# The order of two DMA issues ahead of the first projection, and one more matmul of ones, in a gated-mix kernel

## The chip, the cores and the metric

The kernel runs on one core of one Trainium2 chip. The metric is device time in microseconds (us). The engines are TensorE (PE; its weight loads are shown apart, as PEld), VectorE (DVE), ScalarE (ACT), GpSimd (POOL) and SyncE (SP). SP and ACT issue the DMAs here, each on a queue of its own: in the profile SP's is q1 and ACT's is q10, and both move their packets over the same 16 DMA engines.

## What is computed

Two mixers of a sequence of 2048 tokens of width 512 and a gate between them:

```python
x = A_x                                            # (1, 2048, 512), bf16
g = sigmoid((x * gate_w).sum(-1, keepdims=True))
# A: attention with 32 heads of 16, over 8 earlier tokens at a step of 2
qkv = x @ wqkv                                     # wqkv: (512, 1536)
a = softmax(q . k at positions s, s-2, ..., s-14) @ v, then @ wo
# B: a MLP over tokens
h = layernorm(x)                                   # over the width
u = gelu(einsum("bsd,sf->bdf", h, w1) + b1)        # f = 1792
b = transpose(einsum("bdf,fs->bds", u, w2) + b2)
out = g * a + (1 - g) * b
```

## The kernel before, in words

All of SBUF is one tensor, `arena`, cut into regions: X (x, tokens on the partitions, 16 tiles of 128 tokens), XT (x transposed, four chunks of 128 of the width, 2048 tokens), WQKV, W1W, Q5, K5, V5 and others. PSUM is `ps`, eight banks of 512 columns; banks 0 to 3 are called acc0 to acc3, banks 4 to 7 lg4 to lg7.

PE's work, in order of time: the projections of Q, K and V (L617), the attention's sums over heads (L696, twice), the first layer of the MLP (L810), its second layer (L860) and the output projection (L876). VectorE takes the statistics of the layer norm (L572 on), the products of Q and K (L688), the softmax and the products with V (L795, L798), and the last combination (L897). ACT brings PE's results out of PSUM (L625 and L628 for the projections).

Every operation is given to a small planner (`_Sched`): `add` for an engine's operation, with what it reads and writes, an estimated duration and a priority, and `dma` for a transfer on an engine's queue. The planner sorts each engine's list by estimated start, and puts semaphore waits where one engine's operation depends on another's or on a DMA. `lands` on a DMA is an estimate of when its data is there, for the planner alone; `order` fixes a sequence without a wait. Everything on an engine is then executed in the order of its list.

What the change touches is the start. Time zero is the span's start.

- **ACT's queue.** `d_xp` (line 479, issued by line 429) loads the *plain columns* of block 0: the first 128 columns of x for tokens 0 to 511, into XP, with tokens on the partitions, 128 KB. Behind it `ld_w(0, 0, 1, "act")` (line 481, issued by line 429) loads *Wq's first quarter*: rows 0 to 127 of wqkv, the 512 columns of Q, 128 KB. After these ACT loads a table and does the eviction of line 553.
- **SP's queue.** `ld_xt0` (line 473) loads columns 128 to 511 of x for tokens 0 to 511 with a transposing DMA, 384 KB, into chunks 1 to 3 of XT. Behind it come Wq's second, third and fourth quarter (128 KB each), Wk in two halves (256 KB each), x's first tiles, then the next transposing load (line 460), and so on.
- **PE.** `warm1` is five matmuls of ones by ones with 512 columns, `warm2` one with 256 columns, into bank 7 (line 536; both operands are constants of 1.0 and nothing reads the result; in this text they are the *matmuls of ones*). Then `tr0` and `tr1` (line 544) transpose the four 128 by 128 pieces of XP by a matmul with the identity into banks 5 and 6, and `warm3` is one more of line 536. Bank 5 is brought into chunk 0 of XT by ACT (`ev_tra`, line 553) and bank 6 by VectorE (`ev_trb`, line 555).
- **The first projections** (line 617). They go by quarters of the contracted width: four matmuls of 512 columns, one for each of Q's four column groups, with chunk 0 of XT and Wq's first quarter; then four with chunk 1 and the second quarter; four with chunk 2, four with chunk 3; then sixteen for K in two halves. A step waits for its chunk and its quarter. The first step so needs the plain columns, transposed and evicted, and Wq's first quarter; the second needs `ld_xt0` and the second quarter.

Of the kernel before, what the change touches and what calls it, by code (L numbers as in the profile page):

```python
# [333 lines left out]
def bass_gated_mix__sliding_local_dilated__mixer_token_mlp__prompt_kernel(nc, A_x, A_wqkv, A_wo, B_x, B_w1, B_b1, B_w2, B_b2, gate_w, out, dbg=None):  # L334
    with contextlib.ExitStack() as es:
# [79 lines left out]
        A = sch.add  # L415
# [12 lines left out]
        def mk_dma(dst, src):  # L428
            return lambda e: e.dma_start(dst, src)  # L429
# [3 lines left out]
        def throttle():  # L433
            return [init_dmas[-5]] if len(init_dmas) >= 5 else []

        def prev_dma():
            return [init_dmas[-1]] if init_dmas else []

        def ld_x(t0, n, q="sp"):
            ds = sch.dsem("x%d" % t0)  # L440
            op = sch.dma(q, mk_dma(X[:, t0:t0 + n, :], xv[:, t0:t0 + n, :]), n * 128 * D * 2, ds,
                         writes=["x%d" % t for t in range(t0, t0 + n)], deps=throttle() if q == "sp" else [], after=prev_dma() if q == "sp" else [], name="d_x%d" % t0)
            if q == "sp":
                init_dmas.append(op)
            return op

        def ld_w(tn, d0, n, q="sp"):
            ds = sch.dsem("wqkv%d_%d" % (tn, d0))
            op = sch.dma(q, mk_dma(WQKV[:, d0:d0 + n, tn * D:(tn + 1) * D], wqkv_v[:, d0:d0 + n, tn * D:(tn + 1) * D]),
                         n * 128 * D * 2, ds, writes=["wqkv%d_%d" % (tn, dt) for dt in range(d0, d0 + n)],  # L450
                         deps=throttle() if q == "sp" and n == 4 else [], after=prev_dma() if q == "sp" else [],
                         issue=0.65 if n == 4 else 0.45, name="d_wp%d_%d" % (tn, d0))
            if q == "sp":
                init_dmas.append(op)
            return op
# [14 lines left out]
        def ld_xt0():  # L470
            ds = sch.dsem("xt0")
            dst = XT[:, 1:4, 0:512]
            op = sch.dma("sp", lambda e: e.dma_start_transpose(dst, x2d[0:512, 128:512]), 512 * 384 * 2, ds, issue=1.25,
                         writes=XT0[1:4], after=prev_dma(), name="d_xt0")
            init_dmas.append(op)
            return op

        XP = view("OUTS", BF16, [(128, 4), (1, 128)])
        d_xp = sch.dma("act", mk_dma(XP, xv[:, 0:4, 0:128]), 512 * 128 * 2, sch.dsem("xp"), writes=["outs0"], issue=0.4, name="d_xp")

        first_loads = [ld_w(0, 0, 1, "act"), ld_xt0(), ld_w(0, 1, 1), ld_w(0, 2, 1), ld_w(0, 3, 1), ld_w(1, 0, 2), ld_w(1, 2, 2),
                       ld_x(0, 2)]
        ld_xt(1)
        first_loads.append(init_dmas[-1])
        for op_, t_ in zip(first_loads, (3.4, 4.6, 5.0, 5.4, 5.8, 6.6, 7.4, 8.2, 10.6)):
            op_.lands = t_
            op_.deps.clear()
        d_xp.lands = 3.1
        first_loads[0].order.add(d_xp)
        init_dmas[:] = [first_loads[1]] + first_loads[5:]  # L490
        ld_x(2, 2)
        ld_x(4, 4)
# [7 lines left out]
        def ld_w1(j):  # L500
# [4 lines left out]
            if j < 4:  # L505
# [8 lines left out]
                       writes=["wo"], deps=throttle(), after=prev_dma(), name="d_wo")  # L514
# [4 lines left out]
        for i_, (v_, n_) in enumerate(((B_b1, NFT), (B_b2, NST))):  # L519
            vr = v_.rearrange("(t q j) -> q t j", q=4, j=32)  # L520
            for q_ in range(4):
                sch.dma("sp", mk_dma(psub(BR, 32 * q_, n_, 32 * i_, [(1, 32)]), vr[q_]), n_ * 64, ds_b, reads=["br"],
                        writes=["br_%d_%d" % (i_, q_)], deps=throttle(), after=prev_dma(), name="d_b_%d_%d" % (i_, q_), issue=0.45)
        d_w1.append(ld_w1(3))
        A("dve", lambda e: e.transpose(out=BT, in_=BR), 0.2, reads=["br_%d_%d" % (i_, q_) for i_ in range(2) for q_ in range(4)],
          writes=["btc"], name="t_b")
# [5 lines left out]
        def f_warm(n, w_=D):  # L532
            def fn(e):
                ins = None
                for _ in range(n):
                    ins = e.matmul(ps[:, 7, 0:w_], lhsT=CONE[:, 0:128], rhs=CONE[:, 0:w_], start=True, stop=True)
                return ins
            return fn

        def f_tr(h):  # L540
# [4 lines left out]
                return ins  # L545
            return fn

        A("pe", f_warm(5), 2.13, writes=["lg7_0", "lg7_1"], name="warm1", prio=-100)
        w2_ = A("pe", f_warm(1, 256), 0.2, writes=["lg7_0", "lg7_1"], name="warm2", prio=-100)
        ta_ = A("pe", f_tr(0), 0.215, reads=["outs0", "ident"], writes=["lg5_0", "lg5_1"], after=[w2_], name="tr0", prio=-100)  # L550
        tr_ = A("pe", f_tr(1), 0.215, reads=["outs0", "ident"], writes=["lg6_0", "lg6_1"], after=[ta_], name="tr1", prio=-100)
# [2 lines left out]
          writes=["xt0_0"], name="ev_tra", prio=0)  # L554
        A("dve", lambda e: e.tensor_copy(out=XT[:, 0, 256:512], in_=ps[:, 6, 0:256]), 0.35, reads=["lg6_0", "lg6_1"],
          writes=["xt0_0b"], name="ev_trb", prio=0)
# [76 lines left out]
        for (b0, d0, d1, s0, s1) in ((0, 0, 1, 0, 512), (0, 1, 2, 0, 512), (0, 2, 3, 0, 512), (0, 3, 4, 0, 512), (4, 0, 2, 0, 512), (4, 2, 4, 0, 512)):  # L633
            for b in range(b0, b0 + 4):
# [3 lines left out]
                                 writes=fbn[b], after=[last_main[0]], name="pf_%s%d_%d_%d" % (tnames[tn], dl, d0, s0))  # L638
                last_main[0].order.add(w3_)
        for b, (tn, dl) in enumerate(first):  # L640
            A("act", f_evq(tn, dl, 0, b), 0.52, reads=fbn[b] + (["k5pad"] if tn == 1 else []),
              writes=["%s5_%d_0" % (tnames[tn], dl)], name="ev_%s%d_0" % (tnames[tn], dl), prio=0)
# [7 lines left out]
        for (tn, dl, sb) in seq_proj:  # L650
# [4 lines left out]
                             writes=["acc%d" % bank], after=[last_main[0]], name="pj_%s%d_%d" % (tnames[tn], dl, sb), prio=0)  # L655
            A("act", f_evq(tn, dl, sb, bank), 0.62, reads=["acc%d" % bank] + (["k5pad"] if tn == 1 else ["v5pad"] if tn == 2 else []),
              writes=["%s5_%d_%d" % (tnames[tn], dl, sb)], name="ev_%s%d_%d" % (tnames[tn], dl, sb), prio=0)
# [11 lines left out]
                writes=["xa"] + ["wqkv%d_%d" % (tn, dt) for tn in range(3) for dt in range(4)], name="d_xa")  # L669
        for t in range(NST):  # L670
# [5 lines left out]
          writes=["th"], name="g_tanh", prio=0)  # L676
# [31 lines left out]
        for wh in range(2):  # L708
# [6 lines left out]
            for (dl, c0, nc_) in pieces:  # L715
# [5 lines left out]
                  writes=wr, name="qkm_%d_%d_%d" % (wh, dl, c0), prio=0)  # L721
            rd = sum([pbn(b_) for b_ in bufs], []) + PBX[wh] + ["rp"]
            for wl in range(4):
                qop = A("pe", f_qkr(list(enumerate(bufs)), (wl,)), 0.92, reads=rd, writes=["lg%d_0" % (4 + wl), "lg%d_1" % (4 + wl)],
                        name="qkr_%d_%d" % (wh, wl), prio=-100 + wl, delay=BURST_DELAY)
                A("act", (lambda wh_, wl_: (lambda e: e.activation(out=ATT[:, :, 4 * wh_ + wl_, :], in_=ps[:, 4 + wl_, :].rearrange("p (h c) -> p h c", h=2), func=AF.Copy)))(wh, wl),  # L726
                  0.55, reads=["lg%d_0" % (4 + wl), "lg%d_1" % (4 + wl)], writes=["lw%d" % (4 * wh + wl)],
                  name="lev_%d_%d" % (wh, wl), prio=0)
# [60 lines left out]
        for k_, u in enumerate(USEQ):  # L789
# [7 lines left out]
            for (nm, n_, du) in (("ava", 4, 2.25), ("avb", 2, 1.2)):  # L797
                A("dve", (lambda pv_, n__: (lambda e: e.tensor_tensor(out=pv_[:, 0:n__], in0=pv_[:, 0:n__], in1=pv_[:, n__:2 * n__], op=ALU.add)))(pv, n_),  # L798
                  du, writes=[pn], name="%s_%d" % (nm, u))
# [27 lines left out]
        for ft in range(NFT):  # L827
# [6 lines left out]
              name="gel_%d" % ft, prio=0)  # L834
# [84 lines left out]
        for i in range(NST):  # L919
# [4 lines left out]
            elif i > 1:  # L924
# [6 lines left out]
              name="t1_%d" % i, prio=0)  # L931
# [119 lines left out]
```

## Time and profile before

| | |
|---|---|
| median of 3 runs | 167.92 us (167.65 to 168.38) |
| the profiled execution | 168.55 us |
| its span in the profile | 167.3 us |
| PE busy | 162.1 us, 97% of the span |
| DVE busy | 151.3 us, 90% |
| ACT busy | 75.1 us, 45% |
| first matmul of ones | starts 0.84 us |
| first transposing matmul (L544) | starts 3.33 us |
| first projection (L617) | starts 5.61 us |

Every line of a timeline gives start, length, engine, line, operation and the names of what it writes and reads; in square brackets stands how long the engine idled before it and what ended that. A line with "x9" merges nine instructions in a row. "DMA ... us to landing" counts from the start of the issuing instruction to the last of the DMA's semaphore updates. [...]

### The profile page before, as it was taken

How to read it: one execution, taken by the hardware profiler on the slowest of the kernel's cores; microseconds unless marked ns; L12 is line 12 of the kernel's file. 1: busy time of each engine (PE TensorE's matmuls, PEld its weight loads, DVE VectorE, ACT ScalarE, POOL GpSimd, SP SyncE). 2: the span in 40 equal slices, each digit the busy share in tenths (PEclk: the TensorE clock that was granted, in tenths of full speed). 3: DMA queues.
4: the chain of work that ended last, by engine and by line, in shares of the span. 5: the costliest groups of instructions: out<-in, count | busy, mean ns of one | idle time of the engine just before them, and what ended most of it. 6: DMA issues, size and time to landing. Idle time of an engine off the chain costs nothing.

```text
span 167.3 us, 2136 instructions
## 1 busy us (share of the span) xinstructions
PE 162.1 (97%) x845; PEld 77.5 (46%) x859; DVE 151.3 (90%) x154; ACT 75.1 (45%) x116; POOL 0.7 (0%) x8
## 2 busy tenths in 40 slices
PE   7699999999999999999999999999999999999994
PEld 2355555554454444444444444444444444444463
DVE  1055999999999999999999999999999999999896
ACT  3077688889899818793131121131231321310100
POOL 1000000000000000000000000000000000000000
PEclk9999999999999999999999999999999999999999
DMA  5999999959003846996779926462672570000454
GB/s 135 327 268 216 314 316 290 303 165 308 2 0 97 311 116 179 307 290 155 181 189 340 339 76 142 113 187 71 181 218 83 138 223 0 0 0 0 157 190 159
DMA packets 47625, 29.64 MB, mean 177 GB/s; under 512 B 9856, under 2 KB 46464, under 8 KB 47616
## 3 DMA queue, kind: packets, MB, share of 16 engines
q1 hardware_dynamic: 45120, 24.85, 54.4%
q10 hardware_dynamic: 2496, 4.66, 10.2%
q8 instruction: 7, 0.11, 0.3%
q14 instruction: 2, 0.02, 0.0%
HBM read 21.24 MB, written 2.10 MB: 140 GB/s over the span
## 4 chain that ended last, share of the span: by engine, by line
PE 91%; DMA 3%; DVE 2%; ACT 2%; issue 1%; ACTq 0%
PE ps L860 29%; PE ps L810 29%; PE ps L617 23%; PE ps L876 6%; PE ps L696 4%; DMA arena<-in_A_wqkv_dram 3%; DVE arena L897 2%; ACT L585 1%; ACT arena L628 1%; ACTq L429 0%; ACT arena L585 0%
## 5 line engine op out<-in xcount | busy, mean ns | idle before, releaser
L860 PE MATMUL ps<-arena 128*128 128x512 bf16 x220 | 48.5, 379 | 0.2
L810 PE MATMUL ps<-arena 128*128 128x512 bf16 x219 | 48.2, 379 | 0.4 <-issue 0.2
L617 PE MATMUL ps<-arena 128*128 128x512 bf16 x188 | 41.4, 379 | 1.6 <-DMA arena<-in_A_wqkv_dram 1.3
L688 DVE TENSOR_TENSOR arena<-arena 128x4096 bf16<-128x4096 bf16 (+1 forms) x12 | 35.5, 2998 | 2.5 <-ACT arena L628 2.1
L795 DVE TENSOR_TENSOR arena<-arena 128x8192 bf16<-128x8192 bf16 x8 | 35.0, 4419 | 0.0
L860 PEld LDWEIGHTS ps<-arena 128*128 128x128 bf16 x224 | 21.9, 98 | 26.4
L810 PEld LDWEIGHTS ps<-arena 128*128 128x128 bf16 x224 | 21.8, 98 | 26.6 <-ACT arena L726 0.4
L617 PEld LDWEIGHTS ps<-arena 128*128 128x128 bf16 x192 | 21.6, 113 | 21.5 <-issue 1.8
L928 ACT ACTIVATE arena<-ps,arena 128x512 bf16<-128x512 f32 x16 | 12.5, 778 | 39.4 <-PE ps L860 39.4
L798 DVE TENSOR_TENSOR arena<-arena 128x4096 bf16<-128x4096 bf16 (+1 forms) x16 | 27.0, 1751 | 0.0
L628 ACT ACTIVATE arena<-ps 128x512 bf16<-128x512 f32 x32 | 18.6, 596 | 4.5 <-PE ps L617 4.5
L831 ACT ACTIVATE arena<-ps,arena 128x512 bf16<-128x512 f32 x14 | 9.6, 687 | 22.2 <-PE ps L810 16.6
L572 DVE BATCH_NORM_STATS2 arena<-arena 128x6 f32<-128x512 bf16 x16 | 10.0, 682 | 6.1 <-DMA arena<-in_A_x_dram 6.1
L876 PE MATMUL ps<-arena 128*128 128x512 bf16 (+1 forms) x79 | 14.1, 336 | 0.1
L897 DVE SCALAR_TENSOR_TENSOR arena<-ps,arena 128x512 bf16<-128x512 f32 (+1 forms) x20 | 11.5, 637 | 0.9 <-PE ps L876 0.7
L596 ACT ACTIVATE arena<-arena 128x512 bf16<-128x512 bf16 x16 | 12.2, 804 | 0.0
L625 ACT ACTIVATE arena<-ps 128x512 bf16<-128x512 f32 x16 | 9.0, 597 | 6.2 <-PE ps L617 6.1
L876 PEld LDWEIGHTS ps<-arena 128*128 128x128 bf16 x80 | 7.8, 98 | 6.2
L672 DVE SCALAR_TENSOR_TENSOR arena<-arena 128x512 bf16<-128x512 bf16 x16 | 10.1, 689 | 0.0
L742 DVE TENSOR_TENSOR arena<-arena 128x512 bf16<-128x512 bf16 (+4 forms) x11 | 7.3, 667 | 0.6 <-ACT arena L761 0.2
L696 PE MATMUL ps<-arena 128*32 128x512 bf16 x128 | 7.3, 380 | 0.0
L726 ACT ACTIVATE arena<-ps 128x512 bf16<-128x512 f32 x8 | 4.7, 592 | 4.6 <-PE ps L696 4.6
(42 smaller groups left out, 40.0 us busy)
## 6 DMA issues: line engine op xcount, KB each, us to landing
arena<-in_B_w_dram SPq DMA_DIRECT2D x7, 1024.0 KB, 8.5
arena<-in_B_w_dram SPq DMA_DIRECT2D x8, 896.0 KB, 5.2
arena<-arena ACTq DMA_DIRECT2D x32, 128.0 KB, 2.9
arena<-in_A_x_dram SPq DMA_DIRECT2D x4, 512.0 KB, 6.1
out_dram<-arena SPq DMA_DIRECT2D x14, 128.0 KB, 1.7
arena<-in_A_x_dram SPq DMA_DIRECT2D x1, 1536.0 KB, 7.9
arena<-in_A_wqkv_dram SPq DMA_DIRECT2D x2, 256.0 KB, 3.8
arena<-in_A_x_dram SPq DMA_DIRECT2D x2, 256.0 KB, 3.6
```

Of the source, the lines that this page charges most:

```text
L596: A("act", (lambda t_: (lambda e: e.activation(out=X[:, t_, :], in_=X[:, t_, :], func=AF.Identity, scale=col(RSTD, t_), bias=col(NMR, t_)) ...
L617: ins = e.matmul(ps[:, bank, s0:s1], lhsT=lhsT, rhs=XT[:, dt, sb * 512 + s0:sb * 512 + s1], start=(dt == 0 and s0 == 0), stop=(dt == 3))
L628: return lambda e: e.activation(out=dst, in_=ps[:, bank, :], func=AF.Copy)
L688: return lambda e: e.tensor_tensor(out=PBL[buf][:, :, 512 * c0:512 * (c0 + nc_)], in0=in0, in1=in1, op=ALU.mult)
L696: ins = e.matmul(ps[32 * c:32 * c + 32, 4 + wl, :], lhsT=RP, rhs=PBL[buf][:, wl, c * 512:(c + 1) * 512], start=(dl == 0), stop=(dl == 3), ...
L795: A("dve", (lambda o_, i0, i1: (lambda e: e.tensor_tensor(out=o_, in0=i0, in1=i1, op=ALU.mult)))(pv, in0, in1), 4.4, reads=v_res + ["atx_% ...
L798: A("dve", (lambda pv_, n__: (lambda e: e.tensor_tensor(out=pv_[:, 0:n__], in0=pv_[:, 0:n__], in1=pv_[:, n__:2 * n__], op=ALU.add)))(pv, n ...
L810: ins = e.matmul(ps[:, bank, :], lhsT=W1W[:, slot, st, 128 * e_:128 * e_ + 128], rhs=X[:, st, :], start=(st == 0), stop=(st == NST - 1))
L860: ins = e.matmul(ps[:, bank, :], lhsT=W2S[slot][:, ft, 128 * e_:128 * e_ + 128], rhs=UT[:, ft, :], start=(ft == 0), stop=(ft == NFT - 1))
L876: ins = e.matmul(ps[:, bank, 0:c1 - c0], lhsT=OT[:, t, 128 * i:128 * i + 128], rhs=WO[:, t, c0:c1], start=(t == 0), stop=(t == 3))
L897: A("dve", (lambda i_, b_, c0_, c1_: (lambda e: e.scalar_tensor_tensor(out=T1[:, i_, c0_:c1_], in0=ps[:, b_, 0:c1_ - c0_], scalar=col(G, i ...
L928: A("act", (lambda i_, bank_: (lambda e: e.activation(out=T1[:, i_, :], in_=ps[:, bank_, :], func=AF.Identity, scale=col(OMG, i_), bias=co ...
```

## The change

The two DMAs on ACT's queue change places: Wq's first quarter is issued first and the plain columns behind it. `warm1` gets a sixth matmul of 512 columns. The planner's estimates of landing follow. On DVE, POOL and SP the list of instructions is the same as before, and PE's and ACT's differ in nothing else.

```diff
-        for op_, t_ in zip(first_loads, (3.4, 4.6, 5.0, 5.4, 5.8, 6.6, 7.4, 8.2, 10.6)):
+        for op_, t_ in zip(first_loads, (3.0, 5.2, 5.6, 6.0, 6.4, 7.2, 8.0, 8.8, 11.2)):
             op_.lands = t_
             op_.deps.clear()
-        d_xp.lands = 3.1
-        first_loads[0].order.add(d_xp)
+        d_xp.lands = 3.7
+        d_xp.order.add(first_loads[0])
...
-        A("pe", f_warm(5), 2.13, writes=["lg7_0", "lg7_1"], name="warm1", prio=-100)
+        A("pe", f_warm(6), 2.56, writes=["lg7_0", "lg7_1"], name="warm1", prio=-100)
```

`first_loads[0]` is Wq's first quarter, `d_xp` the plain columns.

## The prediction

> **What bounds the kernel now.** I read the chain that ended last first, in order of time. Columns: start, length, what.
>
> ```profile
> 0.80 0.46 ACTq L429
> 1.25 0.03 issue
> 1.28 4.24 DMA arena<-in_A_wqkv_dram
> 5.52 0.09 issue
> 5.61 8.36 PE ps L617 x38
> ```
>
> The chain starts with ACT's two DMA issues, waits for the second (Wq's first quarter, issued 1.28, landed 5.52), and from 5.61 it is PE almost without a break. The second view, the waits of PE over the whole run, says how much of a shift at 5.61 can be lost later. Columns: total, times, longest.
>
> ```profile
> PE ps L617 <- DMA arena<-in_A_wqkv_dram: 1.3, 1, 1.3
> PE ps L536 <- PEq L1036: 0.8, 1, 0.8
> PE ps L617 <- ACT arena L585: 0.2, 1, 0.2
> PE ps L810 <- issue: 0.2, 1, 0.2
> ```
>
> After 5.61 PE idles only 0.4 us in all, so whatever moves its first projection (L617) moves the end, less 0.4 at most. One of these two idles, behind ACT's L585, depends on VectorE's statistics, which stand in its queue behind a product that waited 2.06 us for ACT's evictions of PE's results (start 15.07): that moves along too. I take 1:1. The third view is the timeline of the first 6 us.
>
> ```profile
> 0.80 0.46 ACTq L429 DMA_DIRECT2D arena<-in_A_x_dram  x1
> 0.80 1.35 SPq L473 DMA_TRANSPOSE arena<-in_A_x_dram  x1
> ...
> 0.84 2.51 PE L536 MATMUL ps<-const-bfloat16-1.0 128*128 128x512 bf16 x6 [0.84 <-PEq L1036]
> ...
> 1.28 0.53 ACTq L429 DMA_DIRECT2D arena<-in_A_wqkv_dram  x1
> ...
> 3.33 0.58 PE L544 MATMUL ps<-arena 128*128 128x128 bf16 x4
> ...
> 3.96 0.42 DVE L555 CAST arena<-ps 128x256 bf16<-128x256 f32 x1 [2.45 <-PE ps L544]
> ```
>
> The plain columns of x are issued at 0.80 and land 2.4 us later (DMA issues of that window), at 3.20; PE transposes them at 3.33; VectorE's copy of the second half is done at 4.38. So that operand of the first projection is ready 1.14 us before the other, Wq's first quarter at 5.52. The change swaps who is first.
>
> The fourth view is the DMA traffic by queue in narrow windows (q10 is ACT's, q1 is SP's; columns: packets, MB, share of 16 engines). First 2.2 to 2.6:
>
> ```profile
> q10 hardware_dynamic: 364, 0.09, 101.1%
> q1 hardware_dynamic: 17, 0.00, 4.8%
> ```
>
> Then 3.0 to 3.4:
>
> ```profile
> q1 hardware_dynamic: 443, 0.11, 126.8%
> ```
>
> Then 3.6 to 4.0:
>
> ```profile
> q1 hardware_dynamic: 187, 0.05, 64.5%
> q10 hardware_dynamic: 82, 0.08, 56.0%
> ```
>
> ACT's first DMA moves nearly alone (its first packets start just before 2.1, the last in 2.80 to 2.85; 528 in all). SP's transposing load, issued at the same 0.80, has its first packet in 2.50 to 2.54. In 2.85 to 3.45 q10 moves nothing: ACT's second DMA, issued in full at 1.81, stands behind the transposing load. It appears in 3.45 to 3.50, and of its 144 packets 99 start before 4.0 and the last in 4.6 to 4.7. It then lands at 5.52. **The second place in ACT's queue costs 2.3 us more than the first** (5.52 against 3.20), far more than the 0.48 us between the two issues.
>
> **The change, part by part.**
>
> (1) Wq's first quarter takes the first place. It was issued with 128 packets at 0.80 instead of 1.28, in front of the transposing load. By the row of the plain columns it lands at about 3.2, and cannot land much before. Nothing then waits for it: worth nothing by itself, because the other operand comes later.
>
> (2) The plain columns take the second place. ACT's first issue gets 0.07 us longer (0.53 against 0.46), so this one starts at about 1.35. Bounds for its landing: low, if it follows the weights without a gap, 2.1 + 0.45 (the weights' eight packets to an engine: 99 packets, the shares of some 12 engines, start within 3.45 to 4.0) + 0.46 (32 packets at the 14.4 ns of q1 alone: 443 packets on 16 engines in 0.4 us) = 3.0 on the first engines, 3.3 on the last, plus 0.37 from last packet to landing (2.83 to 3.20 for the first DMA) = 3.4 to 3.7. High, the landing of the transposing load itself, 0.80 + 4.9 = 5.7, and a few tenths more, because 512 small packets could alternate with other traffic: 32 x 28.8 ns = 0.92 instead of 0.46. I take 5.5: it is the nearest row, the same place in the same queue against the same load. The 128 KB are the same, and 0.46 for 32 small packets to an engine is about the 0.45 of the weights' eight.
>
> [...]
>
> (3) The path behind the columns. From landing to the transposes 0.13 (3.20 to 3.33), to the end of the later eviction 1.05 (3.33 to 4.38), to the first matmul 0.09 (5.52 to 5.61): 1.27 us at the slow clock of the first microseconds. The clock column shows 1.00 throughout, so I read the clock from the rows of L536: weight loads 0.43 us apart at 512 columns, while L617 does nine in 2.10. At the fast clock the four transposes and their drain save between 0 and 0.25 us (half of their row, 0.58, less what a weight load of 0.11 each keeps); I take 0.15, so 1.12. Their evictions' durations (0.38, 0.42) stay. ACT's eviction waits at the head of ACT's queue; behind it there stand only evictions that need the projection anyhow. VectorE's copy stands ahead of the statistics (L572), whose x arrives at 8.9: covered.
>
> (4) One more 512-column matmul of ones: 0.43 us. They end at 3.35 now, at 3.78 then, or some 0.2 less by when the array is free. With columns at 5.5 this lies in a wait and costs nothing. If the columns landed at 3.4, it would delay the transposes by about 0.3.
>
> (5) SP's queue is unmoved, and the bytes ahead of its loads are the same, so the other quarters land as now (the second: 2.22 + 3.8 = 5.98). They are needed four matmuls, 0.86 us, after the first: covered in the forecast.
>
> **Sum.** First projection at 5.5 + 1.12 = 6.6 to 6.65 against 5.61: +1.0 to 1.05. On the profiled execution (168.55 us, span 167.3, 1.25 outside it) that is 169.6. That execution is 0.63 above the median of 167.92; the shift belongs on the median, so **169.0 us**, 0.6% slower. What can be told from no change with this kernel is about 0.5%, 0.84 us. The forecast's own range, for landings of 5.3 to 5.9, is 168.7 to 169.4.
>
> **Rivals.**
>
> *The clock is not up when the projections start (slower still).* Today PE works from 0.84 to 4.34 and pauses 1.26 us; the projections then run at the fast pace. Then PE would work to 3.78 only, pause 1.8 us, do the transposes and one matmul of ones, and pause again. If that no longer suffices, the projections run at 0.43 instead of 0.22 us each until PE has again been busy for about today's 3.5 us: up to 1.75 us more, 169.0 + 1.75 = 170.75. For it: the work before the first pause shrinks from 3.5 to 2.9 us. Against: it is still more than half of any 3.5 us. [...] Chance 0.18.
>
> *The columns land early in the second place (same).* If the weights had been late only through the few engines that came last (45 of 144 packets after 4.0) and the columns escape that, they land 0.4 after 4.0 to 4.1, at 4.5, and the projection starts at 5.7: +0.1, 168.0. With part of it, up to 5.3. Chance 0.2.
>
> *The columns follow the weights without a gap (not slower).* Place: the engines' turn at about 2.5 us. If the columns' descriptors are there before the transposing load's first packet (2.53 today), they go first and land at 3.4 to 3.7. The transposes start at 3.7 to 3.85 and the projection at 4.85 to 5.0. But its second step needs the second quarter and the transposed columns, 5.98, against 6.47 today: only 0.49 us of that counts, 167.4. It decides from a landing of 4.3 on (4.3 + 1.27 = 5.6). For it: the columns' issue starts only 0.07 later than the weights' does today. Against: the weights were passed over by the load even on engines that came free as late as 2.8. To gain over 0.84 us the load itself would also have to land 0.35 earlier, which a first DMA of 128 instead of 512 packets in front of it could bring. Chance 0.17, of it 0.05 beyond 0.84.
>
> **Chances.** Forecast 0.45, clock 0.18, landing between 0.2, early columns 0.17. Slower by over 0.5% (above 168.76): the clock's 0.18 and 0.41 of the forecast's, 0.59. Within 0.5%: 0.04 + 0.2 + 0.12 = 0.36. Faster: 0.05. The range takes in the landing between and the clock, and leaves out most of the early columns (0.15) and a full loss of clock beyond 170.7 (0.04): 167.7 to 170.7.
>
> **What would show it.** In the profile after: the chain begins with the DMA from in_A_x instead of in_A_wqkv; ACT's second DMA lands 4 us or more behind its issue; L544 starts at about 5.6 instead of 3.33 and the first L617 at about 6.6; q10 is again silent at 3.0 to 3.4. If L617's first nine take 3.8 instead of 2.10, the clock is the cause. If L544 starts before 4.4, the forecast is wrong at step (2).

## The result, and the profile after

The changed kernel takes **170.96 us** (median of 5 executions, 168.96 to 171.95) against 168.06 (5, 167.65 to 168.77). The ratio is 1.0128, 95% interval 1.0094 to 1.0163: slower by 1.3%. The ratio leaves out executions over 1.5% above the fastest of their own kernel (here the one of 171.95), so the medians lie further apart than it says.

The profiled execution is the shortest of the five: 168.96 us, span 167.7. Its chain, in order of time (start, length, what):

```profile
0.79 0.39 ACTq L429
1.18 0.03 issue
1.21 3.75 DMA arena<-in_A_x_dram
4.96 0.14 issue
5.09 0.40 PE ps L544 x4
5.49 0.02 issue
5.51 0.44 DVE arena L555
5.95 0.05 issue
6.00 33.00 PE ps L617 x152
38.99 3.57 PE ps L696 x64
```

The chain begins with the plain columns now, second in ACT's queue, which land at 4.96. The transposes, VectorE's copy and the first projection follow one on the other, and L617 starts at 6.00 instead of 5.61. Against the profiled execution of before, that is 0.39 us later; L696 starts 0.41 later (38.58 before) and the span is 0.4 longer. What lies behind the first L696 is as long as before, 128.7 us: the change is made good or bad in the first 39 us.

That explains 0.4 us, not the 2.9 between the medians. A second profile of the same kernel caught an execution of 170.32 us, span 169.1. Its timeline:

```profile
0.84 2.93 PE L536 MATMUL ps<-const-bfloat16-1.0 128*128 128x512 bf16 x7 [0.84 <-PEq L1036]
...
5.24 0.58 PE L544 MATMUL ps<-arena 128*128 128x128 bf16 x4 [1.46 <-DMA arena<-in_A_x_dram]
...
6.34 5.95 PE L617 MATMUL ps<-arena 128*128 128x512 bf16 x22
```

L617 starts 0.34 us later than in the first profile. Then compare the groups of instructions in 6.4 to 8.4 us (after "x", how many run in that stretch, those that only begin or end in it included; then busy us and mean ns of one). This second profile:

```profile
L617 PE MATMUL ps<-arena 128*128 128x512 bf16 x5 | 2.3, 620 | 0.1
```

The first profile:

```profile
L617 PE MATMUL ps<-arena 128*128 128x512 bf16 x12 | 2.8, 381 | 0.3 <-DVE arena L555 0.3
```

Five matmuls instead of twelve. The 512-column matmuls start 0.43 us apart here (their weight loads at 7.17, 7.60 and 8.03; each matmul is drawn 0.62 us long, so two in a row overlap) and 0.22 us apart in the first profile (17 in 3.86 us). PE's *clock* is this document's name for that pace: up, or full, at 0.22, half at 0.43. It is told from the starts alone, since the profile's column of the granted clock shows 1.00 in both. Here it is not up when the projections start, and in the first profile the transposes already ran at the full pace (0.38 us for L544's four, 0.58 here). L696 starts at 40.35, 1.36 us behind the first profile: 0.34 by the start and 1.02 by the half pace. The two executions are 1.36 us apart. Of six executions of the changed kernel five took 170.3 or more. Only the shortest and the one of 170.32 were profiled, so how the longer ones, up to 171.95, lose the rest is not shown.

So one kernel, started alike (seven matmuls of ones from 0.83 and 0.84 to 3.76 and 3.77), had its clock up before 5.1 us in one execution and only after 8 us in the other, where L617's weight loads are 0.43 us apart up to 8.46. What sets that moment, no run here shows.

### The profile page after: what moved, and what is told of

Read it like the earlier page. It is cut to its first block, busy times and chain, and to the rows that moved or that the text cites. A ratio compares the mean times of both kernels' runs of the same rounds, so it can differ in the third digit from the quotient of the medians.

```text
span 167.7 us, 2152 instructions
## 1 busy us (share of the span) xinstructions
PE 163.1 (97%) x860; PEld 77.6 (46%) x860; DVE 151.3 (90%) x154; ACT 75.0 (45%) x116; POOL 0.7 (0%) x8
## 4 chain that ended last, share of the span: by engine, by line
PE 93%; DVE 3%; DMA 2%; ACTq 0%; issue 0%
PE ps L810 29%; PE ps L860 29%; PE ps L617 25%; PE ps L876 6%; PE ps L696 4%; DVE arena L897 2%; DMA arena<-in_A_x_dram 2%; DVE arena L555 0%; PE ps L544 0%; ACTq L429 0%
## 5 line engine op out<-in xcount | busy, mean ns | idle before, releaser
L617 PE MATMUL ps<-arena 128*128 128x512 bf16 x192 | 41.8, 379 | 0.3 <-DVE arena L555 0.3
L617 PEld LDWEIGHTS ps<-arena 128*128 128x128 bf16 x192 | 21.6, 113 | 20.4 <-DVE arena L555 0.6
L696 PE MATMUL ps<-arena 128*32 128x512 bf16 x128 | 7.3, 380 | 0.0
```

Source lines behind the costliest of these rows:

```text
L617: ins = e.matmul(ps[:, bank, s0:s1], lhsT=lhsT, rhs=XT[:, dt, sb * 512 + s0:sb * 512 + s1], start=(dt == 0 and s0 == 0), stop=(dt == 3))
L696: ins = e.matmul(ps[32 * c:32 * c + 32, 4 + wl, :], lhsT=RP, rhs=PBL[buf][:, wl, c * 512:(c + 1) * 512], start=(dl == 0), stop=(dl == 3), ...
```

## The experiments

**Theory after the result:** two losses. The columns land late in the second place of ACT's queue, and PE then pauses so long ahead of the transposes (1.33 us in the first profile, 1.46 in the second) that in most executions its clock comes up late (before 5.1 us in the first, after 8 in the second). **Rival:** the DMAs alone, with landings that differ widely from one execution to the next.

**1. The order alone** (the changed kernel with five leading ones):

```diff
-        A("pe", f_warm(6), 2.56, writes=["lg7_0", "lg7_1"], name="warm1", prio=-100)
+        A("pe", f_warm(5), 2.13, writes=["lg7_0", "lg7_1"], name="warm1", prio=-100)
```

> The two DMAs of ACT swapped as in the changed kernel, with the five leading matmuls of ones of the kernel before. Clock theory (the changed kernel loses 0.4 us by the later columns and, in most executions, some 2 us more because the clock rises late after a longer pause of PE): the pause ahead of the transposes is 0.43 us longer still, so the time is that of the changed kernel or worse, 170.5 to 172, with executions apart by up to 2 us, and where an execution is long, the first nine matmuls of L617 take more than 3 us. DMA theory (the columns land at very different times in different executions, and the ones don't matter): the same 171 as the changed kernel, the first L617 starting at 7 to 9 us in the long executions, at the fast pace.

171.25 us (170.15 to 172.27, 6 executions), ratio 1.0189 (1.0147 to 1.0230). The profiled one, of 170.15 us:

```profile
6.06 6.29 PE L617 MATMUL ps<-arena 128*128 128x512 bf16 x23
```

It starts L617 at 6.06, between the two profiles of the changed kernel, and loses about 1.1 us to the half pace (L696 starts at 40.19 against 38.99). So the swap alone makes the loss. In this execution, the shortest of its six, the start is not late as the rival has it; the longer ones were not profiled. The sixth matmul of ones may help a little; the intervals overlap.

**2. The ones alone** (the kernel before with six):

```diff
-        A("pe", f_warm(5), 2.13, writes=["lg7_0", "lg7_1"], name="warm1", prio=-100)
+        A("pe", f_warm(6), 2.56, writes=["lg7_0", "lg7_1"], name="warm1", prio=-100)
```

> The order of the kernel before, with six leading matmuls of ones. They would end at about 3.78 by the modelled ends instead of 3.35, and the columns land at 3.2. Clock theory: the transposes go 0.3 to 0.45 later, still ahead of the weights that land at 5.5, and PE's work before the pause gets longer: the same as before or up to 0.3 us less, 167.8 to 168.1. DMA theory: the same as before, 168.1.

168.35 us (167.72 to 168.53, 12 executions), ratio 1.0002 (0.9976 to 1.0027): no difference. But none of the 12 took over 168.6, while of 17 executions of the kernel before beside them three took 170.1 to 170.6.

**3. The changed kernel with ten ones, and 4. with nine**, so that PE works until the columns are there:

```diff
-        A("pe", f_warm(6), 2.56, writes=["lg7_0", "lg7_1"], name="warm1", prio=-100)
+        A("pe", f_warm(9), 3.84, writes=["lg7_0", "lg7_1"], name="warm1", prio=-100)
```

(Ten likewise, with 4.27.)

> The changed kernel with ten leading matmuls of ones instead of six, so that PE is busy until about the landing of the columns at 5.0. Clock theory: the clock is up in all executions when L617 starts at about 6.0 to 6.2; 168.4 to 168.8, executions within 0.6 us. DMA theory: no help, 171, executions apart by 2 to 3 us.

> The changed kernel with nine leading matmuls of ones: at the slow pace they end at 0.84 + 9 x 0.43 + 0.21 = 4.9, about when the columns land (4.78 to 5.10 in four profiles), where ten ended at 5.3 and could hold the transposes up by 0.3 to 0.5 us in the executions in which the clock was not yet up. Two-part theory (about 1.2 us of the loss is the columns' late landing, the rest, some 1.6, is the clock rising a window later): 168.8 to 169.4, a little under the 169.39 of ten, and nothing over 170. If the clock were the whole loss: 168.2 to 168.5, as the kernel before. If the ones only helped by chance: 170 to 171.

Ten: 169.39 us (168.97 to 169.99, 6 executions), ratio 1.0082 (1.0054 to 1.0110). Nine: 169.47 (168.92 to 171.24, 12 executions, eleven of them under 169.8), ratio 1.0067 (1.0031 to 1.0102). The profile of nine:

```profile
0.84 4.03 PE L536 MATMUL ps<-const-bfloat16-1.0 128*128 128x512 bf16 x10 [0.84 <-PEq L1036]
...
5.08 0.38 PE L544 MATMUL ps<-arena 128*128 128x128 bf16 x4 [0.22 <-DMA arena<-in_A_x_dram]
...
5.99 6.23 PE L617 MATMUL ps<-arena 128*128 128x512 bf16 x28 [0.30 <-DVE arena L555]
```

L617 starts at 5.99 as in the first profile of the changed kernel, at the full pace (17 matmuls in 3.86 us); that this is now the rule is concluded from the times, since one execution of nine, 171.24, is still long. Work that is thrown away makes the changed kernel faster. Over the kernels before beside each, its median was 2.9 us more; with ten and nine ones it is 1.2 and 1.15 (168.19 and 168.32 beside them). By the ratios the gain is smaller, 0.8 to 1.0 us. That part is put down to the clock: full from the first L617 on in the profile of nine, half in the second profile of the changed kernel. That the clock comes up "a window later", as the expectation for nine has it, no run shows; the profiles show only where the pace changes, before 5.1 and after 8 us. The DMA rival expected no help and is out as the only cause. What is left is put down to the columns' late landing. The profiles bear out 0.4 to 1.0 us of it: L696 starts at 38.98 with nine ones, at 38.58 and 37.99 in the two profiles of the kernel before (experiment 6). The profiled execution of nine, 168.95, is 0.5 under its median, and what makes up that 0.5 is open. My 168.4 to 168.8 for ten was too low, and that ten hold the transposes up, my second guess, is not shown: nine are no better.

**5. The kernel before with fewer ones**, no DMA changed:

```diff
-        A("pe", f_warm(5), 2.13, writes=["lg7_0", "lg7_1"], name="warm1", prio=-100)
+        A("pe", f_warm(3), 1.28, writes=["lg7_0", "lg7_1"], name="warm1", prio=-100)
```

> The kernel before with three leading matmuls of ones instead of five; no DMA and no wait is changed, and L617 can still start at 5.6. Clock theory: PE's work before the projections shrinks from 3.5 to 2.6 us, so most executions lose 1 to 3 us: 169 to 171, with L617 starting at 5.6 and its first nine matmuls taking over 3 us in the long ones. DMA theory: the ones do nothing, 168.1.

170.09 us (169.31 to 170.80, 6 executions), ratio 1.0113 (1.0080 to 1.0146). The timeline, and then the group of 6.4 to 8.4 us here and in the first profile of the kernel before:

```profile
5.64 6.60 PE L617 MATMUL ps<-arena 128*128 128x512 bf16 x21 [1.37 <-DMA arena<-in_A_wqkv_dram]
```

```profile
L617 PE MATMUL ps<-arena 128*128 128x512 bf16 x6 | 2.8, 634 | 0.0
```

```profile
L617 PE MATMUL ps<-arena 128*128 128x512 bf16 x11 | 2.5, 379 | 0.0
```

The start, 5.64, is that of the profile of before (5.61), and L696 starts at 40.52 instead of 38.58. Less idle work beforehand, and nothing else, costs 1.9 us, in this pair of profiles as in the medians. This is the clock by itself: L617's weight loads go 0.43 us apart up to 9.44.

**6. The kernel before, profiled again.** Why do the kernels with ones until 5 us lose over 1 us when their start is only 0.4 later than 5.61?

> A second look at the kernel before, unchanged. If the profiled execution that the prediction started from was a late one (the weights landed at 5.52, while in the kernel with six ones they landed at 4.64), this one shows the weights at about 4.6, L617 at 4.7 to 5.0 with its first matmuls still slow, and a span of 166.4 to 167.0. If 5.5 is the rule for the second place of ACT's queue, L617 starts at 5.6 again.

167.96 us, span 166.7. The DMA issues of its first microsecond and a half, then its timeline and a row of its weight loads:

```profile
arena<-in_A_x_dram ACTq DMA_DIRECT2D x1, 128.0 KB, 2.3
arena<-in_A_wqkv_dram ACTq DMA_DIRECT2D x1, 128.0 KB, 3.2
```

```profile
4.58 7.73 PE L617 MATMUL ps<-arena 128*128 128x512 bf16 x33 [0.30 <-DMA arena<-in_A_wqkv_dram]
```

```profile
8.44 3.17 PEld L617 LDWEIGHTS ps<-arena 128*128 128x128 bf16 x16 [0.58 <-DMA arena<-in_A_wqkv_dram]
```

The weights, second in the queue, land 3.2 us after their issue here (1.28 + 3.2 = 4.5), not 4.2, and L617 starts at 4.58. With six ones the weights took 3.4, in experiment 5 again 4.3. So the execution that the prediction started from had late weights; beside this one, the 6.0 of the changed kernel is 1.4 us later, and L696 (37.99 here, 38.99 there) 1.0 later. Most of the other 0.4 is lost in this execution to Wk's first half: issued at 3.76, it lands at 8.40, and the weight loads wait for it. An earlier first projection so does not move the end by as much.

**7. The changed kernel, profiled again.**

> A second look at the changed kernel, whose other executions took 170.5 to 172. Clock theory: L617 starts at 5.9 to 6.1 again, but its matmuls go 0.43 us apart until some point between 7.5 and 10, and the span is 168.5 to 171. DMA theory: L617 goes at the fast pace at once but starts at 7 or later.

170.32 us: shown with the result. As the clock theory had it, with L617 0.2 us later than expected.

**8. The transposing load moved back**, and **9. held until the columns are there.** What makes the second DMA late?

```diff
-        first_loads = [ld_w(0, 0, 1, "act"), ld_xt0(), ld_w(0, 1, 1), ld_w(0, 2, 1), ld_w(0, 3, 1), ld_w(1, 0, 2), ld_w(1, 2, 2),
+        first_loads = [ld_w(0, 0, 1, "act"), ld_w(0, 1, 1), ld_w(0, 2, 1), ld_w(0, 3, 1), ld_xt0(), ld_w(1, 0, 2), ld_w(1, 2, 2),
```

(The planner's estimates and its list of earlier loads follow.)

> The changed kernel with SP's transposing load issued behind Wq's second to fourth quarter, so that the plain columns, second in ACT's queue, meet plain loads of 1 KB packets. If they are late because each engine first serves a long turn of the transposing load, they land at 3.6 to 4.3, and L544 starts at 3.8 to 4.4. If the second place in ACT's queue is late by itself, they land at 4.8 to 5.0 as in the changed kernel. The time is no test here, since the transposing load itself comes later.

```diff
-        d_xp.order.add(first_loads[0])
+        d_xp.order.add(first_loads[0]); first_loads[1].deps.add(d_xp)
```

> The changed kernel, with SP's transposing load, and all of SP's loads behind it, issued only when the plain columns have landed. ACT's two DMAs then have the engines to themselves. If what holds the columns up is the loads they share the engines with, they land at 3.3 to 3.7, as the lower bound of the prediction (2.1 + 0.45 + 0.46 + 0.37 = 3.4), and L544 starts at 3.8, behind the ones. If the second place in ACT's queue is late by itself, they land at 4.5 or later. The time is no test: all of SP's loads come some 2.7 us later, so 170 to 172.

Moved back, the columns landed 3.3 us after their issue at 1.24, at 4.56, and L544 started at 4.69: between what the two views expected, so this one doesn't decide. With SP's loads held back, they landed 2.3 us after the issue at 1.22, at 3.5 (DMA issues, then the timeline):

```profile
arena<-in_A_x_dram ACTq DMA_DIRECT2D x1, 128.0 KB, 2.3
```

```profile
3.66 0.59 PE L544 MATMUL ps<-arena 128*128 128x128 bf16 x4
```

Second place costs nothing in the one profile in which SP loads nothing at the same time (2.3 us from issue to landing, 2.2 for the first place). It is late through what it shares the engines with: 3.6 to 3.9 us with the transposing load (in the profiles of the swapped order), 3.3 with plain loads, 2.3 alone. (170.23 and 170.71 us, one execution each: both delay SP's loads, so their time says nothing about the columns.) How much of it is the transposing load's alone is not separated, since experiment 9 holds back all of SP's loads.

**10. Both first in a queue**: the kernel before with six ones and Wq's first quarter issued by SP ahead of the transposing load.

```diff
-        first_loads = [ld_w(0, 0, 1, "act"), ld_xt0(), ld_w(0, 1, 1), ld_w(0, 2, 1), ld_w(0, 3, 1), ld_w(1, 0, 2), ld_w(1, 2, 2),
+        first_loads = [ld_w(0, 0, 1), ld_xt0(), ld_w(0, 1, 1), ld_w(0, 2, 1), ld_w(0, 3, 1), ld_w(1, 0, 2), ld_w(1, 2, 2),
```

> The kernel before with six ones, and Wq's first quarter issued by SP ahead of the transposing load, so that columns and weights are each first in a queue. Both should land at 3.1 to 3.5 and L617 start at about 4.7. If the first step is what counts, the time is 0.3 to 0.5 us under the kernel before, 167.7. If the second step counts (it needs the transposing load, now issued 0.5 us later, to land at 5.6 to 5.8) or the clock, it is the same as before, 168.0 to 168.5, without the executions of over 170.

168.61 us (167.98 to 170.37, 12 executions), ratio 1.0018 (0.9983 to 1.0052): the same. The columns landed 3.0 us after their issue instead of 2.3 to 2.4, so L544 started at 3.91 and L617 at 5.02. One execution took 170.37 in spite of six ones, which the expectation had ruled out. From 2.4 to 2.8 us both queues move here (q1 68 packets, 46.7% of the 16 engines; q10 138, 38.7%), where in the profile of before q10 had 364 and q1 17 from 2.2 to 2.6. So in this profile the first DMA of one queue is put down to have slowed the first of the other by 0.6 to 0.7 us.

**11. Ones on both sides of the transposes**, as a version that might beat both:

```diff
-        A("pe", f_warm(5), 2.13, writes=["lg7_0", "lg7_1"], name="warm1", prio=-100)
+        A("pe", f_warm(6), 2.56, writes=["lg7_0", "lg7_1"], name="warm1", prio=-100)
...
-        w3_ = A("pe", f_warm(1), 0.43, writes=["lg7_0", "lg7_1"], after=[tr_], name="warm3", prio=-100)
+        w3_ = A("pe", f_warm(3, 256), 0.64, writes=["lg7_0", "lg7_1"], after=[tr_], name="warm3", prio=-100)
```

> The kernel before with six leading matmuls of ones, and three of 256 columns instead of one of 512 behind the transposes, so that PE pauses little ahead of L617. Clock theory: no execution over 169, median 167.8 to 168.3, since the kernel before lost some 2 us in 3 of 17 and 5 of 17 executions; in executions with early weights the 256 columns more can hold L617 up by 0.1. If the executions over 170 of the kernel before come from a transfer, they stay: 1 or 2 in 6.

168.28 us (167.75 to 168.96, 12 executions), ratio 1.0015 (0.9998 to 1.0032): not faster in the middle. But together with experiment 2, none of 24 executions with six ones in the old order took over 169, while 8 of the 40 of the kernel before beside them took 169.8 to 170.8.

## Why the prediction was right, and where it was not

The direction was right. The range, 167.7 to 170.7, holds the time that the ratio gives (1.0128 x 167.92 = 170.1); the median, 170.96, lies 0.26 above it. The forecast itself, 169.0, was 1.1 us under the ratio's time: the range reached that far only by the clock rival, at a chance of 0.18. Both mechanisms were the right ones; which of them would weigh more was wrong.

- **What bounds the kernel.** Right between the two first profiles: from the first L617 to L696 it was 33.0 us, from there to the end 128.7 us, in both kernels. It does not hold for an earlier start, where Wk decides (experiment 6). What was missed is that the profiled execution of before, 0.63 us above its median, was one with late weights. The prediction noted the difference and did not ask what it was.
- **Step (1)**, the weights at 3.2: they land 2.4 us after 0.79. Right.
- **Step (2)**, the columns at 5.5: mis-sized, 4.96 and 5.10 in the two profiles. Their issue came at 1.21, not 1.35: ACT's first issue became 0.07 us shorter (0.39) and not longer. The row that it took as nearest, the weights' 5.52, is at the late end of a place that also gave 4.5. That they wait for SP's loads is right (2.3 us from issue to landing with SP's loads held back, experiment 9, against 3.8 and 3.9). The stretch in which q10 is silent came sooner than the prediction said. In the changed kernel's first profile q10 starts 2 packets in 2.6 to 3.0, and q1 406; the transposing load itself began sooner (in 2.2 to 2.6, q1 has 72 packets against 17 before). In 3.0 to 3.4 the silence was already ending:

```profile
q1 hardware_dynamic: 387, 0.10, 111.3%
q10 hardware_dynamic: 58, 0.01, 16.3%
```

  and in 3.6 to 4.0 the two queues moved alike:

```profile
q10 hardware_dynamic: 231, 0.06, 65.1%
q1 hardware_dynamic: 223, 0.06, 62.8%
```

  The counts are of all engines together, so how one engine divides its time between the two queues is not shown.
- **Step (3)**, 1.12 us from landing to L617: 1.04 with the clock up (4.96 to 6.00), 1.24 without (5.10 to 6.34), for which the prediction had 1.27. Right. The 0.15 that it took off for the transposes and their drain was an estimate, and no run shows a drain by itself; measured, L544's four took 0.38 us with the clock up and 0.58 without.
- **Step (4)**, the sixth matmul of ones costs nothing: right (1.0002).
- **Step (5)**, the other quarters are covered: right, no wait of PE names them.
- **The sum.** +1.0 to 1.05 was the columns' share; measured, with the clock kept up, +1.15 to 1.2 in the medians and 0.4 to 1.0 in the profiles. That it came out nearly right is luck, since two errors cancel: the landing was put 0.5 too late, and the start it was compared with was up to 1.0 too late.
- **The clock rival** had the price (up to 1.75 us; 0.8 to 1.7 in the middle, 1.02 in the one profile) and a chance of 0.18; it was the case in the one long execution that was profiled and, by their times, probably in five of six. The step that failed is its "against": work in more than half of any 3.5 us was taken to be enough. In the second profile PE works from 0.84 to 3.77 and again from 5.24, and its clock is not up before 8 us; how much work, over what time, keeps it up is not shown; in experiment 5, with less work still, all six executions took over 169.3. The kernel before has executions about 2 us longer too, some fifth of them (8 of the 40, and 5 of the 17 beside experiment 10), which three timed runs did not show. None of these was profiled; that they are the clock is concluded from the six ones, which removed them in the old order (experiment 10, with the weights on SP's queue, had one).

## What to carry to other kernels

A start-up step is worth what it does to the landing of the later of two operands and what it does to PE's pause: ask both, since less work and a longer pause ahead of the first real matmul cost 1.9 us here with no operand later (experiment 5), and the columns' late landing 0.4 to 1.0. Before reasoning from a profiled execution that is off its median, find out what is different in it; a DMA that shares the engines with another may land a microsecond earlier next time, as Wq's first quarter did (4.2 us after its issue in one profile of the kernel before, 3.2 in the next). Idle work for PE until the first operand is there was cheap: the sixth matmul of ones in the old order gave a ratio of 1.0002. In the old order it showed in the worst executions and not in the median; in the changed one it showed in both.

## What the hardware showed that was not expected

- PE's pace differed between executions of one kernel: 512-column matmuls 0.43 us apart until after 8 us in one, 0.22 from the first L617 on in another, while the profile's column of the granted clock shows 1.00 in both, so that column does not tell the pace of the start.
- The landing of the second of two DMAs on ACT's queue: 2.3 us after its issue with nothing beside it, 3.2 to 4.3 (old order) and 3.6 to 3.9 (swapped) beside SP's transposing load.
